# Output rows in buffers of their own, early products of zeros, and first states kept with heads stacked

## The chip, the cores and the metric

The kernel runs on one core of one Trainium2 chip. Times are device microseconds (us) of one execution; a profiled execution also has a span, which runs from its first to its last instruction. The engines are called PE (TensorE; PEld is its weight load, which overlaps its products), DVE (VectorE), ACT (ScalarE), POOL (GpSimd) and SP (SyncE, which issues all transfers here). A name like SPq means the sequencer of an engine: it waits, branches or issues, and the engine itself stays idle.

## What is computed

Two steps in a row: a gated linear attention over 768 tokens for each of 4 batches and 8 heads of width 48, and a feed-forward layer over all 3072 tokens.

```python
# q, k, v, alpha: (4, 8, 768, 48) float32; alpha lies between 0.8 and 1.0
for t in range(S):
    state = alpha[:, :, t, :, None] * state + einsum('bhd,bhe->bhde', k[:, :, t], v[:, :, t])
    y[:, :, t] = einsum('bhd,bhde->bhe', q[:, :, t], state)
x = y.transpose(0, 2, 1, 3).reshape(3072, 384)
h = x @ w_in                       # w_in (384, 2048), float64
out = maximum(0.01 * h, h) @ w_out # w_out (2048, 384), float64; out is float32
```

## The kernel before, in words

**Attention.** The tokens are cut into 24 units of 128 tokens: unit u is block u // 4 of batch u % 4, so units 0 to 3 are the first blocks of the four batches, 4 to 7 the second. A unit works on two heads stacked on the partitions, one at 0 to 47 and one at 64 to 111 (`HB = 64`, `BR = 112`), and on four such pairs side by side. `scans` makes the running product of alpha (L288), a reciprocal of every sixteenth of its columns into a constant tile `seed` (L290; the rest of `seed` stays zero, from a memset on POOL at L277) and a backward scan from it (L294). `scaled_q` and `scaled_k` multiply q and k by these (L313, L321). `scores` makes q times k (L330), `mask_scores` masks it (copy L340 on ACT, selection L341 on POOL) and then takes from the list `scalings` what earlier units left there (L346, POOL). `k_tokens` turns k back (L353, L355). `outputs` adds the old state's part (L368, not in a first block) and the masked scores' part (L374), makes the new products k times v, `kv`, in PSUM (L385) and writes the rows x as a high and a low part (L391, L392). `next_state` forms `us`: a copy of `kv` on ACT in a first block (L404, one for each head of the pair), else the old state W plus `kv` on DVE (L406, one for each head); `us` times the block's decay goes into W on POOL (L346, through `scalings`).

For the first nine units (`u < AHEAD`) alpha, q and k arrive with tokens on the partitions and PE turns them (`transposed`, L258: four 128 by 128 transposes for each of the three); for later units DVE turns them (L262).

**Feed-forward.** Three units make a block of 384 tokens, eight blocks in all (i = 0 to 7); the 2048 inner columns are 16 slices (f = 0 to 15). An item (i, f) is `ffn_in` (nine products into `ph`, L460; then 0.01 times on ACT, L463, into a tile `t`; maximum on DVE, L466; a rounded part `gh` on ACT, L468; the remainder `gl` on DVE, L472) and, three items later (`LAG`), `ffn_out` (nine products into three PSUM banks, one for each unit of the block, L485). After f = 15 `finish` copies each bank to SBUF (L495, ACT) and sends it out (L497, SP). The copy's tile has the name `t`, so it takes its turn in the same two buffers as the `t` of `ffn_in`.

**Weights.** Each f has 786 KB of float64 weights, which are loaded raw (L188, L192) and split into two float32 parts on ACT and DVE (`converting`, L224 to L243). Blocks 0 and 1 run item by item together while this goes on; block 2 and later run with all weights in SBUF, with the remaining units of attention spread between their items.

**Order.** A planner (the tile framework, with its own timing of the instructions) writes the order of every engine: among the instructions that its clock holds ready, the one that stands first in the program goes first. `tc.issue_after(x)` adds that what is made inside comes behind x on x's engine. Each engine then runs its list strictly in order, and a wait in front holds all that is behind it. PSUM tiles of one name share buffers: `ph` has two banks, "a" and "b" three each.

Of the kernel before, what the change touches and what calls it, by code (L numbers as in the profile page):

```python
# [9 lines left out]
F32 = mybir.dt.float32  # L10
# [12 lines left out]
def gated_linear_attn_ffn(ctx, tc, q, k, v, alpha, w_in, w_out, out):  # L23
    nc = tc.nc
# [74 lines left out]
    def w_out_of(f, n):  # L99
        return w_sb[f][:, n, DM:]  # L100
# [12 lines left out]
    def by_token(t):  # L113
        return t[:, 0:H * HB].rearrange("t (h d) -> t h d", h=H)
# [35 lines left out]
        )  # L150

    nc.vector.memset(ones, 1.0)
    for i in (0, 1, 2):
        for t in loads_sb[i]:
            nc.vector.memset(by_token(t)[:, :, D:], 1.0)
    for n in range(max(NL)):
        for i in range(3):
            if n < NL[i]:
                load(n, i)
        load_values(n)  # L160
    make_identity(nc, ident)
    nc.gpsimd.memset(mask, 1.0)
    nc.gpsimd.affine_select(
# [88 lines left out]
    def transposed(u, i, name, **kw):  # L252

        src = loaded(u, i)
        if u < AHEAD:
            ps = banks4()
            for p in range(NP):
                nc.tensor.transpose(ps[:, p, :], by_token(src)[:, 2 * p:2 * p + 2, :].rearrange("t h d -> t (h d)"), ident)  # L258
            return ps
        t = atp.tile([P, NP, C], F32, name=name, **kw)  # L260
        src = src.rearrange("r (p n) -> r p n", p=NP)[:, :, 0:RUN]
        nc.vector.transpose(  # L262
            t.rearrange("r p (j t) -> r p t j", t=T4),
            src.rearrange("r p (t d) -> r p t d", t=T4)[:, :, :, 0:32],
        )
        return t
# [1 line left out]

    xs = {}

    live, masked, sums = {}, {}, {}

    scalings = []


    STEP = 16
    nc.gpsimd.memset(seed, 0.0)  # L277

    def every(t, first):
        return t.rearrange("r p (m s) -> r p m s", s=STEP)[:, :, :, first]  # L280
# [77 lines left out]
    def outputs(u):  # L358
        tb, b = units[u]
        i, j = divmod(u, UPB)  # L360
        pe, qs, ktok = live[u][:3]
        V, W = vals_sb[u % NV], state[b]
        at = i % 3 * (NG + 1)
        y = banks4()

        if tb:
            for p in range(NP):
                nc.tensor.matmul(  # L368
                    y[0:BR, p, :], W[0:BR, p, :], qs[0:BR, p, :], start=p == 0, stop=False, skip_group_check=True
                )  # L370
        for p in range(NP):
            for s, lo, m in ((0, 0, D if tb else HB), (1, HB, D)):
                c = (2 * p + s) * D
                nc.tensor.matmul(  # L374
                    y[lo:lo + m, p, :], V[:, c:c + m], masked[u][s][:, p, :],
                    start=not tb and p == 0, stop=p == NP - 1, skip_group_check=True,
                )
        del masked[u]
        kv = None
        if tb < NC - 1:  # L380
            kv = bank()[:, 0:NP * D].rearrange("d (p e) -> d p e", p=NP)
            for p in range(NP):
                for s, lo in ((0, 0), (1, HB)):
                    h = 2 * p + s
                    made["kv", u] = nc.tensor.matmul(  # L385
                        kv[lo:lo + D, p, :], ktok[:, p, lo:lo + D], V[:, h * D:(h + 1) * D], start=True, stop=True
                    )
        load_values(u + NV)
        live[u] = pe, kv
        xh, xl = (x_sb[0:BR, at:at + NP, n, j * C:(j + 1) * C] for n in (0, 1))  # L390
        made["xh", u] = nc.scalar.copy(xh, y[0:BR])  # L391
        made["x", u] = nc.vector.tensor_tensor(xl, y[0:BR], xh.bitcast(F32), ALU.subtract)  # L392

    def next_state(u):
        tb, b = units[u]
        pe, kv = live.pop(u)
        if kv is None:
            return
        W = state[b]
        us = atp.tile([P, NP, D], F32, name="us")  # L400
        for lo in (0, HB):
            r = slice(lo, lo + D)
            if tb == 0:
                nc.scalar.copy(us[r], kv[r])  # L404
            else:
                nc.vector.tensor_tensor(us[r], W[r, :, r], kv[r], ALU.add)  # L406
            scalings.append((W[r, :, r], us[r], pe[r].broadcast_to([D, NP, D]), ALU.mult))

    def gather(i):

# [61 lines left out]
        made["gl", i, f] = put(ordered, "DVE", lambda: nc.vector.tensor_tensor(gl, t, gh.bitcast(F32), ALU.subtract))  # L472
        return gh, gl

    pos = {}

    def ffn_out(i, f, gs, tag):
        gh, gl = gs
        if f == 0:
            pos[i] = [bank(tag)[:, 0:DM] for _ in range(UPB)]  # L480
        po = pos[i]
        for j in range(UPB):
            js = slice(j * C, (j + 1) * C)
            for n, (gt, wn) in enumerate(((gh, HIGH), (gh, LOW), (gl, HIGH))):
                nc.tensor.matmul(  # L485
                    po[j], gt[:, js], w_out_of(f, wn), start=f == 0 and n == 0, stop=f == NF - 1 and n == 2
                )
        if f == NF - 1:
            finish(i)

    def finish(i):
        for j, po in enumerate(pos.pop(i)):
            tb, b = units[i * UPB + j]
            o = ffp.tile([P, DM], F32, name="t")
            nc.scalar.copy(o, po)  # L495
            r = b * S + tb * C
            nc.sync.dma_start(out[r:r + P, :], o)  # L497

# [206 lines left out]
```

## Time and profile before

| | |
|---|---|
| median of 3 runs | 541.08 us (540.25 to 541.96) |
| the profiled execution | 540.7 us, its span 539.0 us |
| PE busy | 520.6 us (97%) |
| DVE busy | 380.3 us (71%) |
| ACT busy | 234.1 us (43%) |
| POOL busy | 64.5 us (12%) |
| last output landed, by the span | about 1.4 us before the end |

The span is 1.7 us shorter than the profiled execution's own time: that is what lies around it. PE's share is an average over stages: until 71 us PE waits now and then for the other engines and for transfers, from 71 to 158 us and from 182 to 534 us it does not wait at all, and the last 5.3 us hold no work of PE. The profile has a column for the clock that TensorE was granted. It shows 1.00 from the first microsecond on, although the first products stand twice as far apart as later ones of the same shape; for the first 17 us the spacing of the products has to be read instead.

### The profile page before, as it was taken

The numbers are of one execution on the slowest core, as the hardware profiler recorded it, in microseconds if no ns is written. First come the engines' busy times: TensorE is split into PE (matmuls) and PEld (weight loads), VectorE is DVE, ScalarE is ACT, GpSimd is POOL, SyncE is SP. The second block draws the span as 40 slices with busy tenths as digits, with TensorE's granted clock in tenths as the row PEclk, the third lists the DMA queues.
The fourth block names the chain that finished last, engine by engine and source line by source line (L and its number), as shares of the span: only waits on it lengthen the run. The fifth ranks groups of instructions, "written<-read, shape, count | busy, mean of one in ns | idle before, by whom it ended". The sixth has DMA issues, their size and how long they took to land.

```text
span 539.0 us, 9954 instructions
## 1 busy us (share of the span) xinstructions
PE 520.6 (97%) x3742; PEld 497.8 (92%) x3742; DVE 380.3 (71%) x694; ACT 234.1 (43%) x494; POOL 64.5 (12%) x140
## 2 busy tenths in 40 slices
PE   6998899999999899999999999999999999999996
PEld 4787789999998799999999999999999999999995
DVE  6899999999999597875685775775876533333331
ACT  2675665545532543435334343344343344233332
POOL 4445420000000022110110101001100000000000
PEclk9998999999999999999999999999999999999999
DMA  9999954545825343433332422413301010101001
GB/s 146 164 177 184 202 140 131 142 111 134 190 43 144 114 107 85 102 79 103 71 82 58 105 64 61 105 42 99 69 1 40 0 45 1 23 0 45 0 1 49
DMA packets 92981, 46.62 MB, mean 86 GB/s; under 512 B 57856, under 2 KB 90112, under 8 KB 92928
## 3 DMA queue, kind: packets, MB, share of 16 engines
q1 hardware_dynamic: 92928, 45.93, 39.4%
q8 instruction: 31, 0.51, 0.4%
q14 instruction: 22, 0.18, 0.1%
HBM read 38.83 MB, written 4.72 MB: 81 GB/s over the span
## 4 chain that ended last, share of the span: by engine, by line
PE 87%; DVE 5%; DMA 3%; issue 1%; SPq 1%; POOL 1%; ACT 1%; DVEq 0%; ACTq 0%; POOLq 0%
PE ph L460 35%; PE b L485 32%; PE a L330 4%; PE a L485 4%; PE a L374 3%; PE a L368 2%; PE b L258 2%; PE a L353 1%; DMA raw<-in_moe_w_in_dram 1%; DMA out_dram<-t 1%; PE a L385 1%; DVE pc L288 1%; PE b L374 1%; PE a L258 1%; DVE rc L294 1%
## 5 line engine op out<-in xcount | busy, mean ns | idle before, releaser
L460 PE MATMUL ph<-large,w 128*128 128x384 f32 x1152 | 225.6, 338 | 3.1 <-DMA raw<-in_moe_w_in_dram 1.9
L460 PEld LDWEIGHTS ph<-large,w 128*128 128x128 f32 x1152 | 200.5, 188 | 5.4 <-DVE t L466 2.2
L485 PE MATMUL b<-w,gh 128*128 128x384 f32 x672 | 169.6, 340 | 1.3 <-ACT t L495 1.3
L466 DVE TENSOR_TENSOR t<-ph,t 128x384 f32<-128x384 f32 x128 | 70.3, 549 | 86.7 <-ACT t L463 86.3
L485 PEld LDWEIGHTS b<-w,gh 128*128 128x128 f32 x672 | 119.5, 188 | 3.7 <-ACT t L495 1.6
L463 ACT ACTIVATE t<-ph 128x384 f32<-128x384 f32 x128 | 62.6, 489 | 136.7 <-PE ph L460 128.6
L468 ACT CAST gh<-t 128x384 fp32r<-128x384 f32 x128 | 65.7, 513 | 108.2 <-DVE t L466 104.7
L485 PE MATMUL b<-w,gl 128*128 128x384 f32 x336 | 107.3, 336 | 0.0
L472 DVE TENSOR_TENSOR gl<-t,gh 128x384 fp32r<-128x384 f32 x128 | 70.3, 550 | 33.6 <-ACT gh L468 30.0
L485 PEld LDWEIGHTS b<-w,gl 128*128 128x128 f32 x336 | 62.6, 188 | 0.1
L341 POOL TENSOR_SCALAR_AFFINE_SELECT sm<-sm 128x512 f32<-128x512 f32 x33 | 21.9, 676 | 117.6 <-ACT sm L340 100.0
L346 POOL TENSOR_TENSOR small<-us,pe 48x192 f32<-48x192 f32 x40 | 25.5, 637 | 85.2 <-DVE us L406 75.3
L330 PEld LDWEIGHTS a<-qs,ks 48*128 48x128 f32 x312 | 26.0, 191 | 6.5 <-issue 5.2
L330 PE MATMUL a<-qs,ks 48*128 48x128 f32 x312 | 31.0, 289 | 0.9 <-DVE ks L321 0.9
L298 POOL COPY pe<-pc 128x4 f32<-128x4 f32 x24 | 5.7, 240 | 175.3 <-DVE pc L288 175.2
L262 DVE STREAM_TRANSPOSE ks<-small 128x512 f32<-128x512 f32 x15 | 16.6, 1119 | 13.6 <-PE a L353 13.6
L340 ACT COPY sm<-a 128x512 f32<-128x512 f32 x24 | 14.0, 584 | 15.1 <-PE b L330 13.3
L288 DVE TENSOR_TENSOR_SCAN pc<-e,small 128x128 f32<-128x128 f32 x60 | 19.9, 391 | 0.0
L485 PE MATMUL a<-w,gh 128*128 128x384 f32 x96 | 19.5, 335 | 0.0
L294 DVE TENSOR_TENSOR_SCAN rc<-e,small 128x511 f32<-128x511 f32 x15 | 19.1, 1272 | 0.2
L374 PE MATMUL a<-sm,small 128*48 128x128 f32 x256 | 18.1, 277 | 1.1 <-POOL sm L341 1.1
L224 ACT ACTIVATE raw<-raw 128x768 f32<-128x768 f32 x16 | 14.6, 915 | 7.0 <-DMA raw<-in_moe_w_in_dram 7.0
(82 smaller groups left out, 542.5 us busy)
## 6 DMA issues: line engine op xcount, KB each, us to landing
raw<-in_moe_w_out_dram SPq DMA_DIRECT2D x16, 384.0 KB, 4.0
small<-in_v_dram SPq DMA_DIRECT2D x24, 192.0 KB, 3.9
raw<-in_moe_w_in_dram SPq DMA_DIRECT2D x32, 144.0 KB, 4.0
out_dram<-t SPq DMA_DIRECT2D x24, 192.0 KB, 2.0
small<-in_alpha_dram SPq DMA_DIRECT2D x32, 96.0 KB, 2.2
small<-in_q_dram SPq DMA_DIRECT2D x30, 96.0 KB, 2.5
small<-in_k_dram SPq DMA_DIRECT2D x30, 96.0 KB, 2.2
small<-in_alpha_dram SPq DMA_DIRECT2D x30, 80.0 KB, 2.4
```

Of the source, the lines that this page charges most:

```text
L288: nc.vector.tensor_tensor_scan(pc[:, p, :], aT[:, p, :], ones.broadcast_to([P, C]), 1.0, ALU.mult, ALU.mult)
L294: nc.vector.tensor_tensor_scan(flat[2][:, NP * C - 2::-1], flat[0][:, NP * C - 1:0:-1], flat[1][:, NP * C - 2::-1], last, ALU.mult, ALU.add)
L330: nc.tensor.matmul(ss[s][:, p, :], ks[lo:lo + D, p, :], qs[lo:lo + D, p, :], start=True, stop=True)
L341: nc.gpsimd.affine_select(out=sm[s], in_=sm[s], compare_op=ALU.is_ge, fill=0.0, base=0, pattern=[[0, NP], [1, C]], channel_multiplier=-1)
L346: nc.gpsimd.tensor_tensor(*scalings.pop(0))
L374: nc.tensor.matmul(y[lo:lo + m, p, :], V[:, c:c + m], masked[u][s][:, p, :], start=not tb and p == 0, stop=p == NP - 1, skip_group_check=True,
L460: nc.tensor.matmul(ph, w_in_of(f, wn, g), xt[:, g, :], start=n == 0, stop=n == 3 * NG - 1)
L463: put(ordered, "ACT", lambda: nc.scalar.mul(t, ph, 0.01))
L466: put(ordered, "DVE", lambda: nc.vector.tensor_tensor(t, ph, t, ALU.max))
L468: put(ordered, "ACT", lambda: nc.scalar.copy(gh, t))
L472: made["gl", i, f] = put(ordered, "DVE", lambda: nc.vector.tensor_tensor(gl, t, gh.bitcast(F32), ALU.subtract))
L485: nc.tensor.matmul(po[j], gt[:, js], w_out_of(f, wn), start=f == 0 and n == 0, stop=f == NF - 1 and n == 2)
```

## The change

Five edits. The output rows get buffers named `o` instead of `t`, and the middle one of the last block's three copies goes to DVE instead of ACT. For the last block, the products of f = 14 are held back and made together with those of f = 15, bank after bank. `seed` is cleared on DVE at the start, and PE gets products that read it: six at the start, and two behind each second transpose of unit 0 (alpha, q and k: twelve more); their result is never read. In units 0 to 3 the copy `us` is one instruction over both heads of the pair, in a buffer of its own for each batch, it is multiplied by the decay in place on POOL (one instruction more, besides the two into W), and units 4 to 7 add it to `kv` with one instruction instead of two. For that the first head's `kv` takes 64 instead of 48 columns of k.

```diff
@@ -150,6 +150,7 @@
         )
 
     nc.vector.memset(ones, 1.0)
+    nc.vector.memset(seed, 0.0)
     for i in (0, 1, 2):
         for t in loads_sb[i]:
             nc.vector.memset(by_token(t)[:, :, D:], 1.0)
@@ -158,6 +159,15 @@
             if n < NL[i]:
                 load(n, i)
         load_values(n)
+
+    idle = ps_h.tile([P, 512], F32, name="ph")
+
+    def keep_warm(n):
+
+        for _ in range(n):
+            nc.tensor.matmul(idle[:, 0:C], seed[:, 0, :], seed[:, 1, :], start=True, stop=True)
+
+    keep_warm(6)
     make_identity(nc, ident)
     nc.gpsimd.memset(mask, 1.0)
     nc.gpsimd.affine_select(
@@ -255,7 +265,12 @@
         if u < AHEAD:
             ps = banks4()
             for p in range(NP):
-                nc.tensor.transpose(ps[:, p, :], by_token(src)[:, 2 * p:2 * p + 2, :].rearrange("t h d -> t (h d)"), ident)
+                last = nc.tensor.transpose(
+                    ps[:, p, :], by_token(src)[:, 2 * p:2 * p + 2, :].rearrange("t h d -> t (h d)"), ident
+                )
+                if u == 0 and p % 2:
+                    with tc.issue_after(last.ins):
+                        keep_warm(2)
             return ps
         t = atp.tile([P, NP, C], F32, name=name, **kw)
         src = src.rearrange("r (p n) -> r p n", p=NP)[:, :, 0:RUN]
@@ -268,13 +283,12 @@
 
     xs = {}
 
-    live, masked, sums = {}, {}, {}
+    live, masked, sums, dense = {}, {}, {}, {}
 
     scalings = []
 
 
     STEP = 16
-    nc.gpsimd.memset(seed, 0.0)
 
     def every(t, first):
         return t.rearrange("r p (m s) -> r p m s", s=STEP)[:, :, :, first]
@@ -380,10 +394,10 @@
         if tb < NC - 1:
             kv = bank()[:, 0:NP * D].rearrange("d (p e) -> d p e", p=NP)
             for p in range(NP):
-                for s, lo in ((0, 0), (1, HB)):
+                for s, lo, m in ((0, 0, HB), (1, HB, D)):
                     h = 2 * p + s
                     made["kv", u] = nc.tensor.matmul(
-                        kv[lo:lo + D, p, :], ktok[:, p, lo:lo + D], V[:, h * D:(h + 1) * D], start=True, stop=True
+                        kv[lo:lo + m, p, :], ktok[:, p, lo:lo + m], V[:, h * D:(h + 1) * D], start=True, stop=True
                     )
         load_values(u + NV)
         live[u] = pe, kv
@@ -397,14 +411,20 @@
         if kv is None:
             return
         W = state[b]
-        us = atp.tile([P, NP, D], F32, name="us")
+
+        us = atp.tile([P, NP, D], F32, name="us" if tb else f"us{b}", bufs=2 if tb else 1)
+        if tb == 0:
+            nc.scalar.copy(us[0:BR], kv[0:BR])
+        elif tb == 1:
+            nc.vector.tensor_tensor(us[0:BR], dense[b][0:BR], kv[0:BR], ALU.add)
         for lo in (0, HB):
             r = slice(lo, lo + D)
-            if tb == 0:
-                nc.scalar.copy(us[r], kv[r])
-            else:
+            if tb > 1:
                 nc.vector.tensor_tensor(us[r], W[r, :, r], kv[r], ALU.add)
             scalings.append((W[r, :, r], us[r], pe[r].broadcast_to([D, NP, D]), ALU.mult))
+        if tb == 0:
+            dense[b] = us
+            scalings.append((us[0:BR], us[0:BR], pe[0:BR].broadcast_to([BR, NP, D]), ALU.mult))
 
     def gather(i):
 
@@ -472,27 +492,32 @@
         made["gl", i, f] = put(ordered, "DVE", lambda: nc.vector.tensor_tensor(gl, t, gh.bitcast(F32), ALU.subtract))
         return gh, gl
 
-    pos = {}
+    pos, last = {}, []
 
     def ffn_out(i, f, gs, tag):
-        gh, gl = gs
         if f == 0:
             pos[i] = [bank(tag)[:, 0:DM] for _ in range(UPB)]
         po = pos[i]
+        last.append((f, gs))
+
+        if i == NB - 1 and f == NF - 2:
+            return
         for j in range(UPB):
             js = slice(j * C, (j + 1) * C)
-            for n, (gt, wn) in enumerate(((gh, HIGH), (gh, LOW), (gl, HIGH))):
-                nc.tensor.matmul(
-                    po[j], gt[:, js], w_out_of(f, wn), start=f == 0 and n == 0, stop=f == NF - 1 and n == 2
-                )
+            for f, (gh, gl) in last:
+                for n, (gt, wn) in enumerate(((gh, HIGH), (gh, LOW), (gl, HIGH))):
+                    nc.tensor.matmul(
+                        po[j], gt[:, js], w_out_of(f, wn), start=f == 0 and n == 0, stop=f == NF - 1 and n == 2
+                    )
+        last.clear()
         if f == NF - 1:
             finish(i)
 
     def finish(i):
         for j, po in enumerate(pos.pop(i)):
             tb, b = units[i * UPB + j]
-            o = ffp.tile([P, DM], F32, name="t")
-            nc.scalar.copy(o, po)
+            o = ffp.tile([P, DM], F32, name="o")
+            (nc.vector.tensor_copy if i == NB - 1 and j == 1 else nc.scalar.copy)(o, po)
             r = b * S + tb * C
             nc.sync.dma_start(out[r:r + P, :], o)
 
```

## The prediction

> **What bounds the kernel now.** I first read the page's chain of work that ended last, then the busy time of every engine in seven stretches (the bounds are where the chain changes its kind).
>
> ```profile
> span 539.0 us, 9954 instructions
> PE 87%; DVE 5%; DMA 3%; issue 1%; SPq 1%; POOL 1%; ACT 1%; DVEq 0%; ACTq 0%; POOLq 0%
> ```
>
> ```profile
> 3.20:9.80 6.60, 4.64 (x16) 2.69 (x16) 4.41 (x10) 0.00 (x0) 2.86 (x9) 1.00 1.29 173
> 9.80:16.30 6.50, 6.47 (x38) 5.26 (x40) 4.22 (x9) 2.73 (x7) 1.60 (x4) 1.00 1.43 174
> 16.30:71.30 55.00, 49.62 (x594) 42.13 (x593) 52.20 (x100) 36.56 (x84) 26.39 (x46) 0.97 1.06 184
> 71.30:157.70 86.40, 86.40 (x499) 86.40 (x498) 84.99 (x136) 46.02 (x80) 1.21 (x2) 1.00 0.52 127
> 157.70:181.50 23.80, 21.28 (x118) 19.76 (x116) 20.58 (x38) 7.21 (x16) 1.19 (x4) 1.00 0.53 134
> 181.50:533.70 352.20, 352.20 (x2488) 341.50 (x2487) 213.00 (x396) 139.32 (x305) 28.75 (x63) 1.00 0.22 55
> 533.70:539.00 5.30, 0.01 (x1) 0.00 (x0) 0.00 (x0) 0.94 (x3) 0.00 (x0) 0.95 0.34 119
> ```
>
> The columns after a stretch and its length are the busy us of PE, PEld, DVE, ACT and POOL, then clock, DMA share and GB/s. From 71.3 to 157.7 and from 181.5 to 533.7 PE is busy without a break: 438.6 us in which nothing but fewer or shorter products helps, and the change takes none away there. So a gain can come from four places: PE's cold start (up to 16.3 us), DVE, busy for 52.20 of 55.00 us up to 71.3 us, the 2.52 us in which PE is idle around 157.7 to 181.5 us, and the last 5.3 us.
>
> **1. Products of zeros at first.** In the timeline, unit 0's first transposes wait for alpha in two halves, the first scan for all four of them; the four L330 rows are the starts of the scores of units 0 to 3. The other two rows are from the chain: the same four transposes early and late.
>
> ```profile
> 3.20 0.66 PE L258 MATMUL a<-small 128*128 128x128 f32 x2 [3.20 <-DMA small<-in_alpha_dram]
> 4.97 1.37 DVE L288 TENSOR_TENSOR_SCAN pc<-a,small 128x128 f32<-128x128 f32 x4 [3.16 <-PE a L258]
> 5.16 0.53 POOL L277 MEMSET small<- 128x512 f32 x1
> 9.82 0.58 PE L330 MATMUL a<-qs,ks 48*128 48x128 f32 x1 [0.86 <-DVE ks L321]
> 17.56 0.37 PE L330 MATMUL a<-qs,ks 48*128 48x128 f32 x1
> 22.87 0.37 PE L330 MATMUL a<-qs,ks 48*128 48x128 f32 x1
> 27.79 0.37 PE L330 MATMUL a<-qs,ks 48*128 48x128 f32 x1
> ```
>
> ```profile
> 12.84 0.85 PE b L258 x4
> ...
> 24.56 0.44 PE a L258 x4
> ```
>
> Four transposes take 0.85 us at 12.84 and 0.44 us at 24.56: PE runs at half clock at first. From unit 0's scores to unit 1's it takes 17.56 - 9.82 = 7.74 us, from 1 to 2 5.31, from 2 to 3 4.92. In the cold stretch DVE is busy for only 4.22 of 6.50 us, so PE holds it up; from unit 2 on DVE sets the pace. If PE were at full clock from about 9.8 us on, the first two steps would take 4.92 us each: 2.82 + 0.39 = 3.21 us gained.
>
> The price stands ahead of it. A product of 128 columns is two records, each paced like a transpose, so 0.85 / 4 x 2 = 0.43 us cold. The memset of `seed` costs 0.53 us on POOL; on DVE, behind one tiny memset, I put its end at 1.5 us (estimate). Six products then end at 1.5 + 2.6 = 4.1 us; two transposes (0.43), two products (0.85), two transposes (0.43) and the pipe's end (0.1) follow, so the first scan starts near 5.95 instead of 4.97: 1.0 us late, and with it unit 0. Moving L277 off POOL costs nothing: POOL has 3.7 us idle in 3.2 to 9.8.
>
> The other twelve products are not all of zeros. Those beside q and k come in the program after L290 has written reciprocals into `seed`, so they wait for it. The planner can then issue the q and k transposes first and the products behind them; taken so, these eight run between k's transposes and unit 0's scores, where PE has slack (it waits 0.86 us before 9.82). By when does the clock open? In the trace it opened after PE had worked without a break from 9.82 to about 16.2 us, 6.4 us. With products from 1.6 us on, and transposes behind them, that is 8.0 us, before unit 0's scores at 10.8. Term: -3.21 + 1.0 = **-2.2 us**. Bounds: -3.2 (no delay), and +4.1 (all 18 products cold, 7.7 us, ahead of unit 0's scores, less the 1.6 + 1.96 us that PE was idle between 1.6 and 9.8).
>
> **2. First states with heads stacked.**
>
> ```profile
> L406 DVE TENSOR_TENSOR us<-small,a 48x192 f32<-48x192 f32 x30 | 10.4, 347 | 0.4
> ```
>
> ```profile
> 52.39 0.34 DVE us L406
> ...
> 52.76 0.35 DVE us L406
> ...
> 55.39 6.42 DMA raw<-in_moe_w_in_dram
> ...
> 65.00 0.37 DVE us L406
> ...
> 65.50 2.29 POOL small L346
> 67.79 0.06 issue
> 67.85 2.30 POOL sm L341 x2
> ```
>
> A group row by shape and a piece of the chain. Units 4 to 7 lose one L406 each; one over 112 partitions takes as long as one over 48, since both have 192 elements on a partition: 0.35 us of DVE per unit. Units 4 and 5 stand on the chain (DVE is full there): -0.7. In unit 6 only the op at 65.00 goes; POOL follows, with its two multiplications still to do, so I take -0.2 of 0.37. Unit 7 comes where PE sets the end: 0. Term **-0.9 us**, bounds 0 and -1.4 (four times 0.35). Units 0 to 3 lose one copy on ACT (idle 3.8 of 6.5 us there: nothing) and gain a multiplication on POOL, 0.5 us where POOL is idle 4.9 of 6.5 us; if POOL were full, the masked scores behind it would be 0.5 us late four times.
>
> Against this stands the wider `kv`. In all of units 0 to 19, eight of sixteen weight loads of L385 go from 48 to 64 columns.
>
> ```profile
> L385 PEld LDWEIGHTS a<-small,ktok x304: 119/125/168, 16.1 to 384.8; 128*48 128x48 f32 x152
> L374 PEld LDWEIGHTS b<-sm,small x22: 123/125/138, 16.9 to 22.6; 128*48 128x48 f32 x12, 128*64 128x64 f32 x10
> ```
>
> ```profile
> 31.36 0.56 PE L385 MATMUL a<-small,ktok 128*48 128x48 f32 x16
> ```
>
> L374 already mixes 48 and 64 columns, at 123 to 138 ns against a median of 125: between 0 and 13 ns for each of 160 loads, 0 to 2.1 us, if none of it hides behind a product. Sixteen products of L385 take 0.56 us, so there is little to hide behind; but the median doesn't move, so I take **+0.3 us**. [...]
>
> **3. Output rows in their own buffers.** Blocks 0 and 1 end together at 171 to 183 us.
>
> ```profile
> 171.97 4.04 DMA out_dram<-t
> 176.08 0.51 ACT t L495 x2
> 176.59 1.90 DMA out_dram<-t
> ```
>
> ```profile
> 176.62 0.62 PE L485 MATMUL b<-w,gh 128*128 128x384 f32 x2 [1.26 <-ACT t L495]
> 179.73 0.44 PE L460 MATMUL ph<-large,w 128*128 128x384 f32 x1 [0.56 <-DVE t L466]
> ```
>
> The second copy waits 4.04 us until the first output has left its `t`; PE waits 1.26 us for that copy's bank. Then L463 waits 1.90 us for another `t`, DVE's L466 is late, and PE waits 0.56 us. With two `o` buffers the second copy follows the first at once and L463 never waits for an output; but the third copy still waits for the first output's 4.04 us, and is then the late one: its bank is the third that PE needs, three products (0.5 us) later. So of 1.26 + 0.56 = 1.82 us I take **-1.2 us**, bounds 0 and -2.5 (all of PE's idle time in this stretch). At later block ends PE never idles: 0.
>
> **4. The last block bank by bank.**
>
> ```profile
> 533.40 1.24 ACT L495 COPY t<-b 128x384 f32<-128x384 f32 x3 [2.65 <-PE b L485]
> 533.90 1.74 SPq L497 DMA_DIRECT2D out_dram<-t  x3
> ```
>
> ```profile
> DMA to landing us min/median/max: 2.6/2.8/2.8
> ```
>
> ```profile
> DMA to landing us min/median/max: 1.8/1.9/4.0
> ```
>
> The last three outputs are copied from 533.40 on, issued at 533.9 to 534.8 and land 2.8 us later, at 537.6; 1.4 us of end follow. After: bank 0 is complete twelve products (2.1 us) before the last and bank 1 six, so two copies and transfers are done early. The last copy takes one third of its row, 0.48 us, from 533.72 on, with its issue at 534.25, and lands after 1.9 us (the second landing row, 160 to 190 us) to 2.6: 536.15 to 536.85. Term **-1.1 us**, bounds -0.7 and -1.5.
>
> **Sum.** -2.2 - 0.9 + 0.3 - 1.2 - 1.1 = -5.1. Span 539.0 - 5.1 = 533.9; the 1.7 us around it make 535.6 for this execution. The median of the runs is 541.08 against this execution's 540.7, so 0.4 more: **536.0 us**.
>
> **The rivals** (each as a median, from 541.1).
>
> *Transfers hold the first 71 us anyway.* For it: between 9.8 and 16.3 us the DMA share is 1.43, its highest, and the weights at 55.39 take 6.42 us to land. If that landing doesn't move, terms 1 and 2's gain are lost: 541.1 + 0.3 - 1.2 - 1.1 = 539.1. Against it: the mean share from 16.3 to 71.3 is 1.06, so there is room to start earlier, and that load is issued behind unit 5's compute work.
>
> *The wait for outputs only moves to the third copy.* Term 3 is then 0: 537.2.
>
> *The early products wait.* Those beside q and k wait for the reciprocal, and if the planner leaves them between the transposes, q and k wait too; PE idles and the clock opens late. Term 1 is then about -0.7 instead of -2.2 (half of the gain from the clock, less the delay: 3.2 / 2 - 1.0 = 0.6): 537.5.
>
> *Slower: the products queue ahead and buy nothing.* If products of zeros don't count as work for the gate, or open it no earlier than now, term 1 is its bound, +4.1: 541.1 + 4.1 - 2.9 = 542.3. It decides from +2.9 on. For it: the early PE queue is in order, and unit 0's scans already set the pace. Against it: transposes alone kept PE busy while the clock opened, so it seems to be time at work that counts. [...]
>
> **How the numbers follow.** Forecast 0.55; transfers 0.15; third copy 0.13; waiting products 0.09; slower 0.08. The likeliest gives 536.0. Low end: best bounds of terms 1 and 3 with the rest as taken, 536.0 - 1.0 - 1.3, and half of what is left in term 2 and 4 (0.5): about 533.2. High end: the transfers' rival with the load price at 1.4 instead of 0.3: 540.2. This kernel can be told from no change at about 0.3%, 1.6 us: faster is below 539.5, slower above 542.7. The forecast, third copy and waiting products lie below 539.5 but for some of their spread (0.70 of 0.77), the transfers' rival about two thirds (0.10): faster 0.80. Slower than 542.7 needs the last rival at its bound and a dear load: 0.07. The rest, 0.13, is the same.
>
> **What would show it.** Right: unit 1's scores start near 15.7 us and unit 2's near 20.6, with four transposes at 0.44 us by 12 us; unit 0's scores start near 10.8; L406 shows 4 fewer instructions and unit 5's stands alone on the chain; PE's waits for L495 and L466 near 175 to 180 us are gone or under 0.6 us together; after PE's last product there is one copy and one issue, and the end comes near 4.2 us after it instead of 5.3. Wrong: transposes still at 0.85 us after 10 us (no early clock), PE's unbroken stretch still beginning at 71 us (a hidden gain), the third copy with a 4 us wait followed by idle PE, or sixteen L385 products at 0.66 us instead of 0.56.

## The result, and the profile after

The changed kernel takes **544.95 us** (544.75 to 546.31, five runs), against 541.08 us (539.85 to 542.12) for the kernel before: 1.0080 times as long, 95% interval 1.0056 to 1.0105. It is 0.8% slower. The profiled execution has a span of 544.6 us, 5.6 us more than before. The forecast was 536.0 us, with a range of 533.2 to 540.2 us. Ratios, here and below, leave out executions more than 1.5% above the fastest of their kernel (there is one, 548.77 us, of the stacked states alone); the medians hold them.

The page's span and chain by engine, and then two of the stretches that the prediction used (columns as there: stretch, its length, busy us of PE, PEld, DVE, ACT and POOL, clock, DMA share, GB/s):

```profile
span 544.6 us, 10010 instructions
PE 87%; DMA 6%; DVE 2%; SPq 1%; POOL 1%; issue 1%; ACT 0%; DVEq 0%; ACTq 0%
```

```profile
16.30:71.30 55.00, 45.01 (x529) 38.74 (x526) 43.57 (x88) 30.17 (x70) 23.90 (x47) 0.94 0.97 182
157.70:181.50 23.80, 23.19 (x133) 22.87 (x132) 23.55 (x43) 8.50 (x18) 0.57 (x3) 1.00 0.41 97
```

Three readings. From 16.3 to 71.3 us both PE (45.01 against 49.62 us) and DVE (43.57 against 52.20 us) do *less*: neither sets the pace any more, both wait, and transfers have doubled their share of the chain (3% to 6%). From 157.7 to 181.5 us PE's idle time has shrunk from 2.52 to 0.61 us, as the output buffers should make it (other items stand there now, as the kernel runs later; the experiment with the buffers alone settles it). And the early clock came; PE's timeline before, and after:

```profile
6.73 1.09 PE L258 MATMUL a<-small 128*128 128x128 f32 x4
```

```profile
1.57 2.93 PE L168 MATMUL ph<-small 128*128 128x128 f32 x12 [1.57 <-DVE small L153]
...
6.52 0.60 PE L268 MATMUL b<-small 128*128 128x128 f32 x4
...
10.55 0.37 PE L344 MATMUL a<-qs,ks 48*128 48x128 f32 x1
14.94 0.63 PE L268 MATMUL b<-small 128*128 128x128 f32 x4 [1.42 <-DMA small<-in_alpha_dram]
16.87 0.37 PE L344 MATMUL a<-qs,ks 48*128 48x128 f32 x1
21.79 0.37 PE L344 MATMUL a<-qs,ks 48*128 48x128 f32 x1
```

The first row is the first six products of zeros, two records each. Four transposes take 0.60 us at 6.52; before, four took 1.09 us at 6.73. The three L344 rows are the starts of the scores of units 0, 1 and 2: 10.55, 16.87 and 21.79 us, forecast 10.8, 15.7 and 20.6. Up to unit 4 the changed kernel is 1.1 us ahead. Then it falls behind: +1.6 us at unit 5 (39.97 against 38.35), +7.1 at unit 7 (61.25 against 54.12), +8.75 at the feed-forward's items 6 to 33, back to about +3.8 at the items 42 to 50, +4.5 by the last unit, +5.6 at the end of the span.

The place is on ACT's timeline, which nothing in the change seems to touch there. Before (L224 is the first step of the weights' conversion, L340 the copies of the scores):

```profile
33.98 0.59 ACT L340 COPY sm<-a 128x512 f32<-128x512 f32 x1 [0.56 <-PE b L330]
...
36.77 0.93 ACT L224 ACTIVATE raw<-raw 128x768 f32<-128x768 f32 x1
...
46.18 0.59 ACT L340 COPY sm<-a 128x512 f32<-128x512 f32 x1
...
52.78 0.91 ACT L224 ACTIVATE raw<-raw 128x768 f32<-128x768 f32 x1 [3.86 <-DMA raw<-in_moe_w_in_dram]
```

After (the same two are L234 and L354; L405 is the copy of x), with the two products of PE that this holds up:

```profile
36.17 0.88 ACT L234 ACTIVATE raw<-raw 128x768 f32<-128x768 f32 x1 [3.84 <-DMA raw<-in_moe_w_in_dram]
36.95 0.57 ACT L354 COPY sm<-a 128x512 f32<-128x512 f32 x1
...
52.93 0.90 ACT L234 ACTIVATE raw<-raw 128x768 f32<-128x768 f32 x1 [5.12 <-DMA raw<-in_moe_w_in_dram]
53.71 0.59 ACT L405 CAST large<-b 112x512 fp32r<-112x512 f32 x1
54.17 0.60 ACT L354 COPY sm<-a 128x512 f32<-128x512 f32 x1
```

```profile
37.58 0.66 PE L268 MATMUL b<-small 128*128 128x128 f32 x4 [2.22 <-ACT sm L354]
...
55.73 1.09 PE L399 MATMUL a<-small,ktok 128*64 128x48 f32 x16 [6.77 <-ACT ktok L369]
```

The weights are scaled when they were before, at about 36 and 53 us. But the scaling that needs them now stands on ACT's list *ahead* of the score copies of unit 4, and that of the next slice ahead of unit 5's x and unit 6's copies. ACT waits 3.84 and 5.12 us for transfers with copies behind it that are ready, and PE waits for those copies.

### The profile page after: what moved, and what is told of

Same layout as the page of the kernel before. It is cut to its first block, busy times and chain, and to the rows that moved or that the text cites. A ratio compares the mean times of both kernels' runs of the same rounds, so it can differ in the third digit from the quotient of the medians.

```text
span 544.6 us, 10010 instructions
## 1 busy us (share of the span) xinstructions
PE 521.0 (96%) x3778; PEld 502.8 (92%) x3778; DVE 379.1 (70%) x692; ACT 231.3 (42%) x489; POOL 65.8 (12%) x143
## 4 chain that ended last, share of the span: by engine, by line
PE 87%; DMA 6%; DVE 2%; SPq 1%; POOL 1%; issue 1%; ACT 0%; DVEq 0%; ACTq 0%
PE ph L480 36%; PE b L509 32%; PE a L509 4%; PE a L344 4%; PE a L388 3%; DMA raw<-in_moe_w_in_dram 2%; PE a L382 2%; DMA small<-in_alpha_dram 2%; DMA small<-in_q_dram 1%; PE a L399 1%; PE a L367 1%; PE b L268 1%; PE b L388 1%; POOL small L360 1%; SPq L198 1%
## 5 line engine op out<-in xcount | busy, mean ns | idle before, releaser
L355 POOL TENSOR_SCALAR_AFFINE_SELECT sm<-sm 128x512 f32<-128x512 f32 x33 | 23.1, 713 | 118.1 <-ACT sm L354 111.9
L344 PE MATMUL a<-qs,ks 48*128 48x128 f32 x312 | 28.5, 285 | 0.1
L344 PEld LDWEIGHTS a<-qs,ks 48*128 48x128 f32 x312 | 23.9, 187 | 5.0 <-issue 4.4
L354 ACT COPY sm<-a 128x512 f32<-128x512 f32 x24 | 14.0, 583 | 14.3 <-PE b L344 12.0
L399 PE MATMUL a<-small,ktok 128*64 128x48 f32 (+1 forms) x304 | 13.3, 220 | 6.8 <-ACT ktok L369 6.8
L399 PEld LDWEIGHTS a<-small,ktok 128*64 128x64 f32 (+1 forms) x304 | 12.2, 135 | 7.7 <-ACT ktok L369 7.0
```

Source lines behind the costliest of these rows:

```text
L344: nc.tensor.matmul(ss[s][:, p, :], ks[lo:lo + D, p, :], qs[lo:lo + D, p, :], start=True, stop=True)
L355: nc.gpsimd.affine_select(out=sm[s], in_=sm[s], compare_op=ALU.is_ge, fill=0.0, base=0, pattern=[[0, NP], [1, C]], channel_multiplier=-1)
L399: made["kv", u] = nc.tensor.matmul(kv[lo:lo + m, p, :], ktok[:, p, lo:lo + m], V[:, h * D:(h + 1) * D], start=True, stop=True)
```

## Experiments

Theory A: this order is the whole loss. B: the wider state products or the stacking cost it. C: the zero products themselves, or the loads behind them, do. Medians are in us; the ratio is to the kernel before, run beside it (median 540.4 to 541.1).

| kernel | median | ratio (95%) |
|---|---|---|
| zero products alone | 544.46 | 1.0068 (1.0049 to 1.0086) |
| stacked states alone | 541.25 | 1.0007 (0.9990 to 1.0025) |
| output buffers alone | 536.13 | 0.9907 (0.9880 to 0.9933) |
| last block alone | 540.43 | 0.9986 (0.9971 to 1.0001) |
| changed, both scalings held back | 536.66 | 0.9912 (0.9888 to 0.9936) |
| zero products, both scalings held back | 539.27 | 0.9970 (0.9948 to 0.9991) |
| changed, held back, zero products at alpha only | 536.90 | 0.9929 (0.9905 to 0.9952) |
| changed, held back, banks in turn | 536.42 | 0.9900 (0.9871 to 0.9929) |
| no stacking, held back, banks in turn, v behind alpha | 536.18 | 0.9918 (0.9889 to 0.9947) |
| changed, held back, v behind alpha | 536.12 | 0.9910 (0.9891 to 0.9929) |
| changed without stacking, nothing held | 541.93 | 1.0023 (1.0010 to 1.0036) |
| changed, only f1's scaling held back | 537.80 | 0.9949 (0.9931 to 0.9968) |
| changed, f1's scaling one place later | 542.30 | 1.0026 (1.0010 to 1.0041) |
| output buffers and banks in turn alone | 535.04 | 0.9893 (0.9876 to 0.9910) |

### Each part alone

Edits: the hunks of the diff for that part, on the kernel before.

> The kernel before with the zero products alone (seed cleared on DVE, 18 products on zeros, nothing else of the change). Theory A, the order on ACT: with these products on PE's list the planner sets ACT's first scaling of the weight slices f0 and f1 ahead of the score copies of units 4 and 6, and there it waits for weights that land at about 36 us and 53 us; so the scores of unit 8 should start some 4.5 to 6 us late against the kernel before (64.15 us there), though unit 4's start about 1.1 us early, and the time should be 5 to 9 us above the kernel before, more than the whole change costs. Theory B, the wider state products: they are not in this kernel, so it should be 1 to 2 us faster than the kernel before. Theory C, the zero products or the later loads themselves cost (an alpha load issued at 10.2 us in place of 7.45 us): the loss would show by unit 2, and the units after it would keep it without growing.

> The kernel before with the stacked first states alone (one copy of 112 rows, kept a second time, and state products of 64 columns for the even heads). Theory A: ACT's scalings keep their places behind the copies of units 4 and 6, so the time stays within 1 us of the kernel before; the sixteen state products should go from 0.56 us to 0.61 us a unit, which over the about 15 units of the stage that PE bounds is 0.7 us late, against some 0.5 us saved in the first four units. Theory B: the wider products cost 2 us or more, the full loss being 4 us with the gains of the other parts taken off.

> The kernel before with output copies in buffers of their own alone. The forecast's term was -1.2 us (0 to -2.5). In the changed kernel the shift against before falls from +8.75 us to about +3.8 us over items 35 to 40, so if these buffers did that by themselves, this kernel should be 4 to 5 us faster; if they only remove the 1.26 us and 0.56 us for which PE waits there, 1.8 us faster; the rest of the fall would then have come from work that the late stage had put off until there.

> The kernel before with the last two slices of the last block bank by bank and DVE's copy of the middle bank alone. The forecast's term was -1.1 us (-0.7 to -1.5). If the planner again sets the three last products of the three banks at the very end, the third issue stands 1.1 us behind the last product as before, and the time is within 0.5 us of the kernel before, or up to 1.3 us above it where the landings take 4.1 us in place of 2.8 us as in the changed kernel.

**Zero products alone** are 3.5 us slower although unit 4's scores start 1.0 us early (31.73 us): ACT's scalings move ahead, at unit 8 they are 3.8 us late, at the items 6 to 33 5.0 us. Theory A said 5 to 9 us in the time, which was too much: 1.9 us of the 5.0 come back at the end of blocks 0 and 1, which I had not foreseen. There the outputs land after 1.9 to 2.1 us in this profile, in the kernel before the first took 4.0 us, and PE doesn't wait for its bank; why it lands sooner is open. B is refuted as the whole cause: no wider product is in this kernel.

**Stacked states alone** change nothing that can be measured. In the trace one side shows clearly, the price: 1.1 us ahead at unit 9's scores (180.40 against 181.49), 0.3 us ahead at unit 21's (410.13 against 410.45), 0.77 us lost in between, by steps of 0.08 us a unit. The lead itself is not shown to come from the stacking. At unit 4's scores, ahead of the first stacked addition, this execution is already 0.9 us ahead (31.80 against 32.73), since its clock opened earlier: four transposes take 0.66 us at 14.63, in the kernel before 1.12 us at 15.10. The last block alone, whose code is the same up to the end, is 0.5 us ahead at unit 4 and 0.7 at unit 9. PE's sixteen state products of one unit before, and here; and the group of their weight loads here, which had 119/125/168 ns before:

```profile
204.64 0.53 PE L385 MATMUL a<-small,ktok 128*48 128x48 f32 x16
```

```profile
203.56 0.61 PE L385 MATMUL a<-small,ktok 128*64 128x48 f32 x16
```

```profile
L385 PEld LDWEIGHTS a<-small,ktok x304: 119/129/138, 15.2 to 384.4; 128*64 128x64 f32 x81, 128*48 128x48 f32 x71
```

The median of 129 ns lies between two kinds: the loads of 48 columns stay at 125 ns, those of 64 take 138, by the single records. The unit pays 0.08 us for eight of them, 10 ns each.

**Output buffers alone** are 4.8 us faster, four times the term. Two things come together between 157.7 and 200 us. The first row is a stretch of this kernel: PE busy 23.19 us in place of 21.28. The next rows are groups of PE from 157.7 to 200 us and starts of the scores of unit 9, before and then here:

```profile
157.70:181.50 23.80, 23.19 (x144) 22.50 (x143) 23.00 (x43) 9.82 (x23) 1.21 (x4) 1.00 0.50 140
```

```profile
L330 PE MATMUL a<-qs,ks 48*128 48x128 f32 x32 | 4.6, 285 | 0.0
...
181.49 1.16 PE L330 MATMUL a<-qs,ks 48*128 48x128 f32 x8
...
184.34 1.16 PE L330 MATMUL a<-qs,ks 48*128 48x128 f32 x8
```

```profile
L330 PE MATMUL a<-qs,ks 48*128 48x128 f32 x32 | 2.9, 287 | 0.0
...
178.41 1.16 PE L330 MATMUL a<-qs,ks 48*128 48x128 f32 x16
```

Eight records of one head of each pair, or sixteen of both heads, take the same 1.16 us: a first head (partitions 0 to 47) and a second (64 to 111) run side by side when they stand next to each other. Before, the planner issued the two heads of units 9 and 10 apart; that cost 1.7 us (4.6 - 2.9). They stand apart in all five profiles in which the rows go through `t`, and in none of the eleven with buffers named `o`; that the planner does it because the banks come free late is my reading of its rule. In the trace the two of a pair start 6 to 7 ns apart. With the 1.91 us of idle time that is 3.6 us; by the starts in the trace 1.3 us more lies in the 138 feed-forward products of the items 34 to 41, on average 179 ns apart in place of 189.

**The last block alone** is at most a gain of 0.5 us that the interval doesn't tell from nothing: its third issue stands 1.1 us behind the last product, as before.

### The order held

```diff
-        with nullcontext() if lines["ACT"] else behind("hi", f - 1):
+        first = behind("sm", 4 + 2 * f) if f < 2 else nullcontext()
+        with first, nullcontext() if lines["ACT"] else behind("hi", f - 1):
             put(ordered, "ACT", lambda: nc.scalar.mul(...
```

> The changed kernel with ACT's first scaling of the slices f0 and f1 held behind the copies of units 4 and 6, where the kernel before has it; nothing else is different. Theory A (the order on ACT is the whole loss): the items 6 to 33 of the feed-forward part come out within 1.5 us of the kernel before in place of 8.75 us behind it, the output buffers take off 5 us behind them, and the time is 534 to 538 us. Theory B (the wider products, or the stacking) or theory C (the zero products and the loads behind them): 543 us or more, since both are still in it.

> The kernel before with the zero products alone, and ACT's first scaling of f0 and f1 held behind the copies of units 4 and 6. Theory A: the loss of 5.0 us at the items 6 to 33 that the zero products alone brought is gone and the 1.0 us gained by unit 4 is left, so 539 to 541 us. Theory C: still 543 us or more.

ACT's timeline of the changed kernel with the scaling held back (its lines are one further down):

```profile
32.64 0.59 ACT L355 COPY sm<-a 128x512 f32<-128x512 f32 x1 [0.55 <-POOL rc L308]
...
36.25 0.91 ACT L235 ACTIVATE raw<-raw 128x768 f32<-128x768 f32 x1 [0.87 <-DMA raw<-in_moe_w_in_dram]
...
49.19 0.59 ACT L355 COPY sm<-a 128x512 f32<-128x512 f32 x1 [0.16 <-PE b L345]
...
51.84 0.94 ACT L235 ACTIVATE raw<-raw 128x768 f32<-128x768 f32 x1
```

The scaling starts when it did (36.25 against 36.17, 51.84 against 52.93), so the weights are no later for it, and unit 4's copies are 4.3 us earlier. The time falls from 544.95 to 536.66 us: 8.3 us for the place of two instructions and for what the planner moved with them, some instructions of DVE, ACT and PE. With the zero products alone it falls from 544.46 to 539.27 us, and that pair is cleaner: by the traces the two scalings are all that differs on ACT, POOL and SP, with one product of q moved on DVE and three neighbouring records on PE. Theory A holds; C falls, since all zero products and late loads are in both kernels. The items 6 to 33 came out 2.3 us behind before in this profile, a little outside the 1.5 us that I gave; in the others with the order held they lie 1.3 us ahead to level. Executions of nearly the same lists thus differ here by up to 3.6 us. A part of that goes with the clock. This profile is of the longest of the kernel's six runs (539.55 us), and its granted clock from 41 to 54 us is 0.77, against 1.00 with the zero products alone, held back:

```profile
41.00:54.00 13.00, 11.75 (x120) 10.74 (x120) 9.76 (x18) 4.95 (x11) 4.78 (x7) 0.77 0.99 186
```

Of its runs the three up to 536.3 us have a mean clock of 0.997 to 0.999, the three from 537.0 us on 0.988 to 0.994.

### Which of the two scalings, and why the stacking matters

Edits: the same condition for f = 1 alone; `behind("xh", 5)` for f = 1 alone; and the changed kernel without the stacking's hunks.

> The changed kernel without the stacked first states, ACT's scalings left where the planner puts them. The parts tried alone add up to 1.4 us faster and the whole is 3.9 us slower: 5.2 us more than the sum. If the stacking makes the difference, because it moves f1's scaling ahead of unit 5's xh copy as well (it stays behind it with the zero products alone), this kernel takes 538.5 to 541 us; if the difference lies elsewhere, 544 us or more.

> The changed kernel with only f1's scaling held behind unit 6's copies; f0's stays ahead of unit 4's copies, where it waited 3.84 us. From the shifts of the changed kernel (1.6 us at unit 5 and 6, 7.1 us at unit 7) f0's place should cost 1.5 to 3 us and f1's 5 to 6 us: so 538 to 540 us here, between 536.7 us with both held back and 545 us with neither.

> The changed kernel with f1's scaling held behind ACT's xh copy of unit 5, one place later on ACT's list and still ahead of unit 6's copies, as the zero products alone leave it; f0's stays where the planner puts it. The changed kernel took 544.95 us, the same without the stacking 541.93 us, and their ACT lists differ there in this one place. If the place is what makes the stacking dear, this kernel takes 541 to 543 us; if the stacking itself costs it (its copies, its wider products), it stays at 544 us or more.

Holding f1 alone brings 7.1 of the 8.3 us; f0's place is the other 1.1 us (537.80 against 536.66; by the ratios 2 us, with intervals that overlap; my 538 was a little too high). The parts tried alone add up to -1.4 us and the whole is +3.9 us. Without the stacking the whole is 3 us shorter (541.93 us; I had expected at most 541), and with the stacking kept but f1's scaling moved behind unit 5's x, one place, it takes 542.30 us. So the stacking costs 3 us beside the zero products mainly by moving one instruction of ACT over another (a few of DVE and a pair of conversions at 72 to 74 us moved with it). ACT's timeline in that kernel:

```profile
47.59 0.58 ACT L406 CAST large<-b 112x512 fp32r<-112x512 f32 x1
...
52.05 0.90 ACT L235 ACTIVATE raw<-raw 128x768 f32<-128x768 f32 x1 [3.89 <-DMA raw<-in_moe_w_in_dram]
52.86 0.56 ACT L355 COPY sm<-a 128x512 f32<-128x512 f32 x1
```

Unit 5's x is written at 47.59 us in place of 53.71, and the gather of its block needs that. The other 2 us of the 5.2 are, by the shifts, of the same stretch as the buffers' gain: 1.9 us of the zero products' loss came back at the end of blocks 0 and 1 without the buffers, so with them there was that much less to win.

### What holds the start

Edits: products only behind alpha's transposes (`u == 0 and i == 0 and p % 2`); and the loads of v for units 1 and 2 made behind the load of alpha for unit 2.

> As the changed kernel with the scaling held back, and the four groups of zero products behind q's and k's transposes left out (only those ahead of everything and behind alpha's stay). If those products hold SP's load of alpha for unit 2 (issued at 10.20 us in the changed kernel, 7.45 us before), it is issued ahead of 9 us here, PE's wait of 1.42 us for it shrinks to under 0.5 us, and the scores of units 2 to 4 start 0.5 to 1.2 us earlier than with all the zero products. If the clock closes for want of them, the scores of unit 0 take 1.5 us longer and nothing is gained.

> The changed kernel with the scaling held back (536.66 us) and SP's loads of v for units 1 and 2 held behind the load of alpha for unit 2. Leaving out q's and k's zero products did not move that load (10.03 us); in SP's list of the changed kernel two loads of v of 1.2 us each stand ahead of it that stand behind it in the kernel before. If they are what holds it, it is issued at 7.4 to 8 us, PE's wait of 1.4 us for it shrinks below 0.5 us and the scores of units 2 to 4 start 0.8 to 1.4 us earlier than with the scaling held back alone (21.54 us for unit 2). If the buffer holds it, it stays near 10 us.

SP's timeline of the changed kernel, then of the one with fewer zero products, then PE's and SP's of the one with v behind alpha:

```profile
6.42 3.66 SPq L147 DMA_DIRECT2D small<-in_v_dram  x3
10.20 0.95 SPq L128 DMA_DIRECT2D small<-in_alpha_dram  x1
```

```profile
10.03 0.95 SPq L128 DMA_DIRECT2D small<-in_alpha_dram  x1
```

```profile
7.63 1.03 SPq L128 DMA_DIRECT2D small<-in_alpha_dram  x1
...
15.38 0.37 PE L345 MATMUL b<-qs,ks 48*128 48x128 f32 x1
...
18.32 0.66 PE L269 MATMUL a<-small 128*128 128x128 f32 x4 [1.25 <-DMA small<-in_k_dram]
...
21.66 0.37 PE L345 MATMUL a<-qs,ks 48*128 48x128 f32 x1
```

Fewer zero products don't move alpha's load (10.03 us): that expectation fell. The last sentence of the expectation came in part. PE is then idle for 1.88 us ahead of unit 0's scores, and these fall to half pace after half a microsecond:

```profile
10.55 0.37 PE L345 MATMUL a<-qs,ks 48*128 48x128 f32 x1 [1.88 <-DVE ks L336]
...
11.00 0.42 PE L345 MATMUL a<-qs,ks 48*128 48x128 f32 x1
```

From 11.00 us on the scores of one bank start 0.21 us apart, in the kernel with all the zero products 0.11 us; the granted clock from 11 to 14 us is 0.50 against 1.00. Unit 0's scores take 0.6 us longer and unit 1's start at 16.98 us in place of 16.61. So the products beside q and k, which are not of zeros, hold the clock open. The time (536.90 us) does not show it.

Two loads of v that the planner had put ahead of it hold alpha's load; with them behind, it is issued at 7.63 us and unit 1's scores start at 15.4 us, as the forecast had it (15.7). But unit 2's start at 21.66 us, no earlier than without (21.54), where 0.8 to 1.4 us had been expected: now PE waits 1.25 us for k. Its load is issued 0.3 us later than with the scaling held back alone (12.34 against 12.00 us) and lands 1.3 us later (18.27 against 16.93). In the traces the loads land one behind the other, mostly 1.1 to 1.2 us apart, also the first four, which SP issues some 0.5 us apart; and the seventeenth lands at 22.4 to 22.9 us in each of the five profiles that I compared, the kernel before among them. So it looks like the pace of the transfers, and not the order of SP's issues, that sets unit 2's start at some 21.6 us in every order tried. The time (536.12 us) shows no gain.

### The end, and a faster version

Edit, in `ffn_out`, with the scaling held back: each bank's last products behind those of the bank ahead.

```diff
-                    nc.tensor.matmul(
+                    with behind("po", j - 1) if len(last) > 1 else nullcontext():
+                        made["po", j] = nc.tensor.matmul(
```

> As the changed kernel with the scaling held back, and the last products of each bank of the last block held behind those of the bank ahead, so that the banks really end one after another (1.03 us apart, six products of 0.17 us). The last gl was there at 534.1 us in the changed kernel, so PE should not wait. The third issue should stand 0.55 to 0.65 us behind the last product in place of 1.11 us, and the span should end 3 to 3.6 us (landing 2 us) or 5 to 5.7 us (landing 4.1 us) behind that product's start of copy, in place of 5.3 us before and 6.6 us in the changed kernel.

PE and ACT at the end of the changed kernel, then its landings, then the same of this one:

```profile
537.36 0.68 PE L509 MATMUL b<-w,gl 128*128 128x384 f32 x3
537.73 0.86 ACT L520 COPY o<-b 128x384 f32<-128x384 f32 x2 [4.21 <-PE b L509]
537.90 0.56 DVE L520 COPY o<-b 128x384 f32<-128x384 f32 x1 [3.79 <-PE b L509]
538.24 1.31 SPq L522 DMA_DIRECT2D out_dram<-o  x3
```

```profile
DMA to landing us min/median/max: 1.9/4.1/4.1
```

```profile
527.28 0.48 ACT L522 COPY o<-b 128x384 f32<-128x384 f32 x1 [2.48 <-PE b L511]
...
527.79 2.41 SPq L524 DMA_DIRECT2D out_dram<-o  x3
...
528.99 0.34 PE L511 MATMUL b<-w,gl 128*128 128x384 f32 x1
529.37 0.48 ACT L522 COPY o<-b 128x384 f32<-128x384 f32 x1 [1.60 <-PE b L511]
```

```profile
DMA to landing us min/median/max: 2.0/2.1/4.2
```

In the changed kernel the three last `gl` products still stand together at the end, although `gl` was there at 534.1 us. Held in turn, the third issue stands 0.54 us behind the last product in place of 1.11, as expected, and PE doesn't wait. The last landing took 4.2 us, and the span ends 6.0 us behind the start of that copy, later than the 5 to 5.7 us that I gave for such a landing: no better in this profile. In all sixteen profiles the third transfer took between 2.8 and 4.2 us to land, a spread wider than the whole term; in the three with the banks in turn the first two took 1.9 to 2.1 us and the third 3.7 to 4.2.

> The changed kernel without the stacked first states, with the two scalings held back, the last block's banks one after another, and SP's loads of v for units 1 and 2 held behind the load of alpha for unit 2. If the parts add: 541.1 us less 1.7 (zero products with the order held) less 4.8 (output buffers) less 0.5 (last block) less 0.5 to 1 (alpha's load) = 533 to 534 us. If the start is bound by the weights' transfers instead, what the start gains is lost by the items 6 to 33 and the time is 535.5 to 537 us, as with the output buffers alone (536.1).

> The kernel before with output buffers of their own, DVE's copy of the middle bank, and the last block's banks one after another; no zero products and no stacking. Output buffers alone took 536.13 us. With the third issue 0.5 us earlier behind the last product this should take 535.3 to 536.1 us, no worse than all the parts together with the order held (536.2 us): then the early products and the stacking are worth nothing once the buffers are there.

All parts in their best order, without the stacking, take 536.18 us: the gains don't add, the second expectation. Output buffers and banks in turn, nothing else, take **535.04 us**, 0.9893 of the kernel before, a little below what I expected; what the banks in turn add to the buffers is not shown, since the intervals overlap (0.9876 to 0.9910 and 0.9880 to 0.9933). Once the buffers are there, no gain of the zero products and the stacking can be shown, in any order.

## Why the prediction was wrong, point by point

**The step that failed is term 1's price, and with it the sum.** The zero products were costed on PE's queue alone: their delay, a gain of 3.21 us, a worst case of all 18 ahead of unit 0's scores. ACT's and SP's lists were taken as they stood. But a planner that times its instructions writes them, and 18 products on PE change its times. The runs put +8.3 us on the new place of two ACT instructions (5.2 us with the zero products alone), in a stage that the term didn't reach. None of the rivals had it: "products queue ahead" was a price on PE, and the early products did not wait for the reciprocal in a way that hurt (without them unit 0's scores start at 10.55 us too). The planner issued q's and k's transposes first, as taken.

With the order held the whole change takes 536.66 us, near the forecast's 536.0. That is luck and not the sum come true: the buffers alone give 4.8 us where it had 1.2, and of the other terms' 3.9 us no gain beside the buffers can be shown.

**Term 1 itself** (-2.2 us): the clock opened by 6.5 us, earlier than my 8.0, and unit 0's delay was 0.73 us (1.0 forecast), but by unit 2 only 1.1 us were gained, because the loads set the start there. Some of that is the execution's luck: in the other profiles without zero products unit 2's scores start between 21.94 and 23.12 us, against 22.87 in the one compared with. With the order held the zero products alone are worth 0.3% (541.07 to 539.27 us, 1.8 us). In that profile they are only 0.3 us ahead at the items 6 to 33, no more than the last block alone (0.4); 1.8 us come at the end of blocks 0 and 1, where the outputs landed after 1.9 to 2.1 us again, the first in the kernel before after 4.0. Whether the zero products shorten that landing is open. The rival that transfers hold the start was right about the place, and I gave it 0.15. An argument against the last rival was misread, too: it was not "transposes alone" that kept PE busy while the clock opened before, since the scores (L330) and the masked scores' products (L374) stand between 9.82 and 16.2 us as well.

**Term 2** (-0.9 us, +0.3 us): the early gain is not shown (of the 1.1 us at unit 9, 0.9 were there at unit 4, ahead of the first stacked addition); the wider products took 0.08 us a unit, 0.77 us between units 9 and 21, and would take an estimated 1.6 us if PE set the pace in all 20, not 0.3 us. "The median doesn't move" was the wrong row to go by: the load of 64 columns took 138 ns against 125, 13 ns more, and little of it hid behind a product (10 of the 13 ns showed in PE's time); the upper end of the 0 to 2.1 us for the loads was nearer. The addition over 112 partitions took 339 ns in the changed kernel (median of four) against 357 ns for one over 48 before, so that the time of the instruction was taken right. Nothing is left of the term in the time.

**Term 3** (-1.2 us, bounds 0 and -2.5): right in mechanism for the idle time, but the measured 4.8 us are four times the term and outside its bounds. PE's idle time fell by 1.91 us, so the third copy's wait did not take its place; the pairs of heads that came together again (1.7 us) were not in the sum at all, since I had counted PE's idle time and not what PE did while it was busy.

**Term 4** (-1.1 us): failed as built. "Bank 0 is complete twelve products before the last" read the program's order; the planner undid it. And 1.9 to 2.6 us were taken for a landing that took up to 4.2 us.

**The signs in "what would show it"**: the transposes, unit 0's scores and the waits for L495 came as forecast; unit 1's and 2's scores, the single copy after the last product and the end 4.2 us behind it (6.6 us) did not. None of them looked at ACT between 33 and 56 us.

## What to carry to other kernels

Where a planner orders the engines, the cost of an edit includes the lists of engines that it doesn't touch: compare every engine's order before pricing anything, and look for a waiting instruction that moved ahead of ready ones. An instruction that waits for a transfer should be tied behind the work that must not wait for it, as the two scalings should have been from the start. Measure each part alone: here one of the four parts held the whole gain, and the sum of the parts was 5.2 us off.

## What the runs showed of the hardware that I had not expected

Products of zeros open the clock: transposes ran at full pace (four in 0.60 us) about 5 us after the first zero product (1.57 to 6.5 us); over the eleven profiles with these products the full pace begins between 4.8 and 7.6 us, in the five others between 13.9 and 16.3. And the clock fell again in an idle stretch of PE: in the changed kernel the granted clock is 0.50 from 53.9 us on, inside the 6.77 us wait that ends at 55.73, up to 60.8 us (0.52 from 54 to 61 us), so the wait cost more than its length.

```profile
54.00:61.00 7.00, 5.27 (x43) 4.56 (x44) 3.48 (x6) 3.19 (x9) 3.13 (x4) 0.52 0.82 175
```

Between the opening and the last products the clock stood at 0.50 twice in the changed kernel, for 6.8 us from 53.9 us on and for 3.4 us from 77.8 us on, and once in the kernel before, for 3.4 us from 50.4 us on. With fewer zero products the pace halved after 1.88 us without a product. How long PE has to be idle for the clock to fall is not shown.

The clock also goes with the order on ACT over all runs: in the four kernels in which f1's scaling stands ahead of copies that are ready, the median of the runs' mean clock is 0.985 to 0.989, in the other twelve 0.992 to 0.997. So part of the 8.3 us was lost while PE worked, at half clock; how much is not separated.

The same 192 KB output transfer took 1.9 to 4.2 us to land at the end of a kernel, with no other transfer issued beside the last three; why is open.
